# A gated mix of a spectral filter and a dense layer: first weights by halves, exchange writes on two queues, a new order, last stores moved

## The chip, the core and the metric

The kernel runs on one core of a Trainium2 chip. Five engines work side by side, each on its own list of instructions: TensorE (PE, matmuls; its weight loads are shown as PEld), VectorE (DVE), ScalarE (ACT), GpSimd (POOL) and SyncE (SP, which here only issues transfers and waits). Semaphores order them. The metric is the device time of one execution in microseconds (us). A profiled execution gives a trace; its span runs from the first to the last instruction.

## The reference

Inputs are bfloat16; S = 2048 rows, D = 512 columns, F = 1792 features. Two branches are mixed by a gate for each row:

```python
x = A_x
y = irfft2(rfft2(x) * (A_w_r + 1j * A_w_i))    # A: spectral filter
h = x @ B_w1 + B_b1
b = (h * tanh(softplus(h))) @ B_w2             # B: dense, Mish, dense
g = sigmoid((x * gate_w).sum(-1))
out = g * y + (1 - g) * b
```

Both branches read the same x.

## The kernel before

Everything is made as a list of tasks (`_Graph.add`), each with an engine, an assumed duration, what it reads and writes, and a priority. `schedule` (L203) simulates the engines with these durations and writes out one fixed order for each engine: among the tasks that could start within 0.03 us of the earliest, it takes the one of highest priority, with a small random term from `SEED`. Loads named in `LAND` (L334) are taken to land at the times in that table, others by size and a tail. `run_engine` (L918) then emits every engine's list in this order, with a semaphore wait ahead of a task for each thing that it needs. An engine never passes a waiting task.

The rows are 16 tiles of 128 (x's row 16p + t is partition p of tile t). The stages, with their lines:

- Loads (L487 to L523): x by tiles, w1 by feature tiles, constants, w2 and the filter W. SP and ACT issue the early ones in turn, POOL the bias, w2 and W, each queue in order.
- Warm-up matmuls on a zeroed buffer (L484), then transposes of x (L534) by way of PSUM, copied to xT by DVE (`evx`, L459).
- The dense branch. `mm1` (L855): 4 chunks of 4 row tiles, 14 feature tiles each, 4 matmuls of 128x512 for each feature tile; Mish on ACT (L862) empties the PSUM bank; `mm2` (L879): 14 matmuls for each row tile, done in two parts of 7. The banks that a chunk may use are in `DENSE` and `DENSE2`.
- The spectral branch. A1 (L572) and the combines into Abuf (L464) are a transform along d. `s1` (L603), four steps over 4 row tiles each, and its copies `e2` (L459 on DVE, L460 on ACT) into Ybuf are the first half of the one along rows. Exchange 1 writes Ybuf to a scratch in DRAM (`r1w`, 16 writes of 128 KB, L614) and reads it back with rows and partitions rearranged (`r1r`, 4 reads of 512 KB, L683), which waits for all writes. `s2` (L744), the filter's products on DVE (`wm`, L464) and sums on POOL (`wz`, L464), and `s2i` (L775) follow. Exchange 2 (L786, L791) and `s1i` and `a1i` (L804, L816) go back.
- A few filter columns have a chain of their own: `wcols` on POOL (L640), `rcw` on PE (L649), `weff` on DVE (L656), `wab1` and `wab2` on POOL (L662, L669); later `s2c` (L699), `crv`, `rcc` (L717).
- The gate (L621 on DVE, the power on POOL at L626) and the mix: `bev` (L837) scales mm2's result, `sum` adds; for the last two row tiles `fin` (L891) does both from PSUM. Stores go to SP's queue in pairs of tiles (L842), tile 14 alone, tile 15 in two halves of 256 columns (L894).

At the end SP waits for every load that it has not waited for yet (L943), then for the stores (L944).

Of the kernel before, what the change touches and what calls it, by code (L numbers as in the profile page):

```python
# [7 lines left out]
BF = mybir.dt.bfloat16  # L8
# [5 lines left out]
NT = 16  # L14
# [87 lines left out]


def _kind(name):
    return name.split("_")[0] if "_" in name else name.rstrip("0123456789")
# [47 lines left out]
class _Graph:  # L153
# [49 lines left out]
    def schedule(self):  # L203
# [13 lines left out]
        rng = np.random.RandomState(SEED)  # L217
        prio = {id(t): t.prio + OFFS.get(_kind(t.name), 0.0) + NOISE * rng.uniform(-1, 1) for t in tasks}
# [8 lines left out]
        while left:  # L227
# [92 lines left out]
NBF = 14  # L320
# [3 lines left out]
S1B = [(6, 7), (4, 5)]  # L324
A1B = (3, 4, 5, 6, 7)
SEED = 1294
NOISE = 0.02
OFFS = {}
SPEC = (3, 4, 5, 6, 7)
DENSE = {0: (0, 1, 2), 1: (0, 1, 2), 2: (0, 1, 7), 3: (0, 1)}  # L330
DENSE2 = {0: (0, 1), 1: (0, 1), 2: (0, 1, 2, 7), 3: (0, 1, 2, 7)}
NWARM = 16
COLD = 4.5
LAND = dict(ld_x0=2.8, ld_x1=3.0, ld_x2=3.5, ld_x3=3.7, ld_w1_0_0=5.6, ld_w1_0_1=5.2,  # L334
            ld_fd=5.8, ld_b1=4.7, ld_w1_2_0=7.6, ld_w1_2_1=7.2, ld_x4=9.1, ld_x6=8.4,
            ld_w1_4_0=10.6, ld_w1_4_1=9.9, ld_x8=11.9, ld_m10=13.2, ld_x12=14.5, ld_w1_8_0=15.2,
            ld_w1_8_1=15.9, ld_m11=17.3, ld_w1_12_0=17.7, ld_w1_12_1=18.1, ld_gw=18.4, ld_sm=20.1,
            ld_gd=20.3)
# [3 lines left out]
def _build(nc, A_x, A_w_r, A_w_i, B_x, B_w1, B_b1, B_w2, gate_w, out):  # L342
# [8 lines left out]
    with es:  # L351
# [76 lines left out]
        def dma(name, dst, src, reads=(), writes=(), nbytes=0, deps=(), is_out=False, prio=None, queue="sp", bw=380e3, tail=1.1, nd=128, issue=0.62):  # L428
            t = G.add(name, queue, 1.0 if queue == "pool" else issue, lambda e: e.dma_start(dst, src),  # L429
                      reads=reads, writes=writes, lat=tail, deps=deps, prio=prio)  # L430
            t.xfer = nbytes / bw
            t.isdma = True
            t.nd = nd
            if is_out:
                t.sem = out_sem
                n_out_dma[0] += 1
                t.semval = 16 * n_out_dma[0]
            else:
                t.sem = new_sem("d_" + name)
                t.semval = 16  # L440
            return t
# [28 lines left out]
        t_id = G.add("ident", "pool", 0.3, lambda e: e.affine_select(out=ident[:, :], in_=ident[:, :], pattern=[[1, 2], [2, 64]],  # L470
# [6 lines left out]
        G.add("wz", "dve", 0.3, lambda e: e.memset(act[:, 2, 0, :], 0.0), writes=["warm"])  # L477
        G.add("ebz", "pool", 0.2, lambda e: e.memset(b1f[:, 0:1], 0.0), writes=["b1z"])
        t_tab = G.add("table", "act", 1.3, lambda e: e.activation(b1f[:, 1:2], b1f[:, 0:1], AF.Mish), reads=["b1z"], writes=["b1t"], prio=0.0)

        pw = _Ps([6])
        tw = []
        for i in range(NWARM):
            tw.append(pe(f"warm{i}", mm(256), lambda e: e.matmul(ps[:, pw.bank, 0:256], act[:, 2, 0, 0:128], act[:, 2, 0, 0:256], start=True, stop=True),  # L484
                         reads=["warm"], alloc=pw if i == 0 else None, frees=[pw], prio=0.0, deps=tw[-1:]))
# [10 lines left out]


# [3 lines left out]
        ld_w1(0, 2, both)  # L501
        dma("ld_fd", FDs[:].rearrange("p r k -> p (r k)"), d_FD[:], writes=["FD"], nbytes=131072)
        dma("ld_b1", braw[:, :], B_b1.rearrange("(ft p) -> ft p", p=128), writes=["braw"], nbytes=3584, queue="pool", deps=[t_id])
        ld_w1(2, 4, both)
        ld_x(4, 6)
        ld_x(6, 8, "act")
        ld_w1(4, 8, both)
# [9 lines left out]
        for h in range(2):  # L517
            dma(f"ld_w2_{h}", w2_sb[:, 7 * h:7 * (h + 1), :], w2v[:, 7 * h:7 * (h + 1), :],
                writes=[("w2", h)], nbytes=128 * 7 * 1024, queue="pool", deps=[t_sm], bw=270e3)
        for i in range(2):  # L520
            for g in range(4):
                dma(f"ld_W{i}{g}", WT[32 * g:32 * g + 32, i, :, :].rearrange("p r k -> p (r k)"), Wv[i][g],
                    writes=[("W", i, g)], nbytes=32 * 8224, queue="pool", deps=[t_sm], bw=230e3)  # L523
# [3 lines left out]
        for t0, w in ((0, 1), (1, 1), (2, 2), (4, 2), (6, 2), (8, 2), (10, 2), (12, 2), (14, 2)):  # L527
            pt = _Ps(SPEC[::-1])
            def f_tr(e, t0=t0, w=w, pt=pt):
                ins = None  # L530
                for i in range(w):
                    for c in range(4):
                        o, d0 = (c * w + i) * 128, 256 * (c // 2) + c % 2
                        ins = e.transpose(psb[:, pt.bank, o:o + 128], xo[:, t0 + i, d0:d0 + 255:2], ident[:, :])  # L534
                return ins

            pe(f"tr{t0}", 4 * w * mm(128), f_tr, reads=[("x", t0 + i) for i in range(w)] + ["ident"], writes=[("ptr", t0)], alloc=pt)
            evict(f"evx{t0}", 512 * w, lambda t0=t0, w=w: xT[:, :, 128 * t0:128 * (t0 + w)],
                  lambda pt=pt, w=w: psb[:, pt.bank, 0:512 * w].rearrange("p (c j) -> p c j", c=4), rate=2.0,
                  reads=[("ptr", t0)], writes=[("xT", t0 + i) for i in range(w)], frees=[pt], engs=("dve",))  # L540
            if t0 == 2:
                pb = _Ps(SPEC[::-1])
                pe("tr_small", 0.1, lambda e, pb=pb: e.transpose(psb[:, pb.bank, 0:14].rearrange("p (a b) -> p a b", b=2), braw[0:14, :],
                                                                    ident[0:14, :].rearrange("p (b a) -> p a b", b=2)[:, 0:7, :]),
                   reads=["braw", "ident"], writes=["ptb"], alloc=pb)
                G.add("ev_small", "dve", 0.2, lambda e, pb=pb: e.tensor_copy(out=b1f[:, :], in_=psb[:, pb.bank, 0:14]),
                      reads=["ptb", "b1t"], writes=["b1f"], frees=[pb])
# [3 lines left out]
        for t in range(NT):  # L551
# [39 lines left out]
            if t % 4 == 3:  # L591
# [17 lines left out]
                for tp, p1 in zip((t - 3, t - 1), p1s):  # L609
                    evict(f"e2_{tp}", 1024, lambda tp=tp: Y1[:, 2 * tp:2 * tp + 4, :].rearrange("p (i b) k -> p i b k", b=2),  # L610
                          lambda p1=p1: ps[:, p1.sl, :].rearrange("p b (i k) -> p i b k", i=2),
                          reads=[("p1", tp)], writes=[("Y1", tp)], frees=[p1], prio=PR["sp"] + E2P, engs=("act",) if tp % 4 else ("dve",))
                    for rho in range(2):
                        dma(f"r1w{tp}{'ab'[rho]}", scr1_w[rho][:, 2 * tp:2 * tp + 4, :], Y1[rho::2, 2 * tp:2 * tp + 4, :], reads=[("Y1", tp)],  # L614
                            writes=[("scr1", tp, rho)], nbytes=64 * 4 * 512, prio=PR["sp"] + 1.0, tail=0.5, bw=300e3)
# [66 lines left out]
        for v in range(4):  # L682
            dma(f"r1r{v}", In2[:, 2 * v:2 * v + 2].rearrange("p u g k -> p (u g k)"),  # L683
                scr1_r[:, 2048 * v:2048 * v + 2048], reads=S1R, writes=[("In2", rho, 2 * v + i) for i in range(2) for rho in range(2)], deps=s1_tasks,
                nbytes=128 * 4096, prio=PR["sp"] + 1.0)
# [155 lines left out]
        def store(t):  # L841
            dma(f"out{t}", ov[:, t - 1:t + 1, :], xo[:, t - 1:t + 1, :], reads=[("o", t - 1), ("o", t)],  # L842
                nbytes=128 * 2048, is_out=True, prio=PR["fin"], tail=0.6)

        mm2s = {}
        for c in range(NCH):
            hb = c % 3
            G.cur_prio = PR["mm1"] - c
            for ft in range(NFT):
                pd = _Ps(DENSE[c])  # L850

                def f_mm1(e, c=c, ft=ft, pd=pd):
                    ins = None
                    for i in range(4):
                        ins = e.matmul(ps[:, pd.bank, :], w1_sb[:, i, 128 * ft:128 * (ft + 1)], xT[:, i, 512 * c:512 * c + 512],  # L855
                                       start=(i == 0), stop=(i == 3))
                    return ins

                pe(f"mm1_{c}_{ft}", 4 * mm(512), f_mm1, reads=[("xT", 4 * c + i) for i in range(4)] + [("w1", ft, 0), ("w1", ft, 1)],
                   writes=[("pm", c, ft)], alloc=pd, deps=mm2s.get(c - 3, ()), prio=PR["mm1"] - c - 0.06 * ft)  # L860
# [4 lines left out]
                      reads=[("pm", c, ft), "b1f"], writes=[("act", hb, ft)] + (["warm"] if hb == 2 and ft == 0 else []), frees=[pd], prio=PR["mish"])  # L865
            G.cur_prio = PR["mm2"] - c
            for tl in range(4):
                t = 4 * c + tl

                for part in range(2):  # L870
                    if part == 0 or t == NT - 1:
                        pd = _Ps(DENSE2[c])
                    cs_ = slice(256 * part, 256 * part + 256) if t == NT - 1 else slice(0, 512)
# [9 lines left out]
                    tk = pe(f"mm2_{t}_{part}", 7 * mm(512), f_mm2,  # L883
# [4 lines left out]
                    if t < NBF or (t < NT - 1 and part == 0):  # L888
                        continue
                    G.add(f"fin_{t}_{part}", "dve", dve_dur(256 if t == NT - 1 else 512, True),  # L890
# [4 lines left out]
                        nbytes=65536 * (1 if t == NT - 1 else 2), is_out=True, prio=PR["fin"], tail=0.6)  # L895
# [22 lines left out]
        def run_engine(ename, eobj):  # L918
            seen = {}
            for t in order[ename]:  # L920
                need = {}
# [18 lines left out]
            if ename == "sp":  # L940
                for t in G.tasks:
                    if t.isdma and t.sem is not out_sem and seen.get(t.sem.num, 0) < t.semval:
                        eobj.wait_ge(t.sem, t.semval)  # L943
# [67 lines left out]
```

## Time and profile before

| | us |
|---|---|
| three runs, median (lowest to highest) | 132.81 (132.79 to 133.22) |
| the profiled execution | 132.8 |
| its span | 131.1 |
| PE busy, share of the span | 124.9, 95% |
| first transposes on PE | 3.81 |
| first dense matmul (L855) | 7.29 |
| first step of s1 (L603) | 33.56 |
| first s2 (L744) | 54.45 |
| last s2i (L775) | 83.09 |
| first s1i (L804) | 93.59 |
| end of PE's last matmul | 128.15 |

The starts are those of the chain of work that ended last and of the timeline; all are us from the span's start. About 1.7 us of the execution lie outside the span. In the profile a line such as `7.29 1.89 PE L855 MATMUL ... x8 [0.79 <-DVE Tg L464]` gives the start, the time from the first start to the last end, the engine and line, the number of instructions, and in brackets the idle time before and what is thought to have ended it. A transfer's row gives the time from its issue to its landing.

### The profile page before, as it was taken

To read this page: it belongs to the slowest core of one execution; us is meant where nothing else is said; L and a number is where in the kernel's file an instruction comes from. 1 tells how busy PE (TensorE), PEld (TensorE's weight loads), DVE (VectorE), ACT (ScalarE), POOL (GpSimd) and SP (SyncE) were. 2 spreads that over 40 slices of the span, in tenths; PEclk is the share of its full clock that TensorE was granted. 3 is DMA by queue.
4 is the path that set the end of the run, shared out by engine and by line. 5 is a ranking of instruction groups with operands and counts; after the bars stand their busy time and mean duration, and the time that the engine had idled before them with its cause. 6 is when DMAs were issued, how large, how long until landed. Compare 5 with 4: busy or idle time off the path is not lost.

```text
span 131.1 us, 2497 instructions
## 1 busy us (share of the span) xinstructions
PE 124.9 (95%) x930; PEld 64.9 (50%) x947; DVE 89.3 (68%) x159; ACT 72.2 (55%) x119; POOL 58.3 (44%) x89
## 2 busy tenths in 40 slices
PE   6979999999999999999999999999999999999991
PEld 4646666544454444344343333344566555555580
DVE  0437989979797941296498994500267996899691
ACT  0437557898878787621236867922347741562420
POOL 6000009700020774059479979100019676879710
PEclk9999999999999999999999999999999999999999
DMA  3899964999956544956104050466910042022213
GB/s 106 258 293 420 386 209 81 368 287 228 223 138 199 171 123 109 336 235 250 75 26 134 3 160 5 143 177 171 404 70 0 0 156 84 5 80 83 80 46 116
DMA packets 16892, 21.09 MB, mean 161 GB/s; under 512 B 1200, under 2 KB 13360, under 8 KB 16496
## 3 DMA queue, kind: packets, MB, share of 16 engines
q1 hardware_dynamic: 14736, 15.95, 36.4%
q0 software_dynamic: 896, 3.94, 11.8%
q10 hardware_dynamic: 1248, 1.05, 2.6%
q8 instruction: 7, 0.11, 0.4%
q14 instruction: 5, 0.04, 0.1%
HBM read 14.64 MB, written 6.29 MB: 160 GB/s over the span
## 4 chain that ended last, share of the span: by engine, by line
PE 94%; issue 2%; DVE 1%; ACT 1%
PE ps L855 37%; PE ps L879 37%; PE ps L534 4%; PE ps L603 3%; PE ps L804 3%; PE ps L572 3%; PE ps L816 3%; PE ps L484 2%; PE ps L744 2%; PE ps L775 1%; ACT act L862 1%; DVE Tg L464 1%; DVE xo L891 0%; DVE act L477 0%; PE ps L699 0%
## 5 line engine op out<-in xcount | busy, mean ns | idle before, releaser
L855 PE MATMUL ps<-xT,w_sb 128*128 128x512 bf16 x214 | 51.0, 380 | 1.6 <-DVE Tg L464 0.8
L879 PE MATMUL ps<-w_sb,act 128*128 128x512 bf16 (+1 forms) x231 | 50.4, 366 | 0.4
L862 ACT ACTIVATE act<-ps,b1f 128x512 bf16<-128x512 f32 x56 | 38.5, 687 | 14.9 <-PE ps L855 14.1
L879 PEld LDWEIGHTS ps<-w_sb,act 128*128 128x128 bf16 x238 | 22.4, 98 | 22.1 <-issue 0.6
L855 PEld LDWEIGHTS ps<-xT,w_sb 128*128 128x128 bf16 x224 | 20.0, 98 | 25.5 <-ACT act L862 2.5
L464 POOL TENSOR_TENSOR Tg<-Qb 128x256 bf16<-128x256 f32 x29 | 21.6, 772 | 20.8 <-DVE Qb L827 20.8
L837 ACT ACTIVATE xo<-ps,omg 128x512 bf16<-128x512 f32 x14 | 9.6, 687 | 25.7 <-PE ps L879 22.9
L464 POOL TENSOR_TENSOR Zb<-Qb 128x510 bf16<-128x510 f32 x16 | 19.9, 1269 | 8.3 <-DVE Qb L464 8.3
L464 DVE TENSOR_TENSOR Qb<-ps,WT 128x1024 f32<-128x1024 f32 x16 | 18.8, 1218 | 6.3 <-PE ps L744 5.5
L827 DVE SCALAR_TENSOR_TENSOR Qb<-ps,gcol,Qb 128x256 f32<-128x256 f32 x32 | 13.6, 474 | 2.5 <-PE ps L816 2.5
L459 DVE CAST Ybuf<-ps 128x1024 bf16<-128x1024 f32 x8 | 9.8, 1220 | 4.6 <-PE ps L775 2.9
L464 DVE TENSOR_TENSOR Abuf<-ps,Tg 128x512 bf16<-128x512 f32 x16 | 10.3, 684 | 3.6 <-ACT Tg L579 3.6
L459 DVE CAST Zb<-ps 128x512 bf16<-128x512 f32 x7 | 4.7, 688 | 11.6 <-PE ps L804 11.2
L621 DVE SCALAR_TENSOR_TENSOR Tg<-xo,Tg 128x512 bf16<-128x512 bf16 x16 | 11.0, 686 | 0.3
L821 ACT ACTIVATE Qb<-ps,gcol 128x256 f32<-128x256 f32 x16 | 7.2, 470 | 7.0 <-PE ps L816 7.0
L429 POOL DMA_DIRECT2D w_sb<-in_B_w_dram x2 | 1.9, 974 | 16.9 <-DMA sm<-c_sm 16.9
L464 DVE TENSOR_TENSOR xo<-xo,Tg 128x512 bf16<-128x512 bf16 x14 | 9.3, 690 | 0.2 <-ACT xo L837 0.2
L460 ACT ACTIVATE Ybuf<-ps 128x1024 bf16<-128x1024 f32 x8 | 8.2, 1023 | 1.5 <-PE ps L603 1.2
L459 DVE COPY xT<-ps 128x1024 bf16<-128x1024 bf16 (+1 forms) x9 | 5.4, 627 | 4.6 <-PE ps L534 4.4
L640 POOL COPY wrv<-WT 128x2 bf16<-128x2 bf16 x2 | 0.4, 187 | 12.8 <-DMA WT<-in_A_w_i_dram 12.8
L804 PE MATMUL ps<-m1g,Abuf 128*128 128x128 bf16 x64 | 5.7, 219 | 0.0
L816 PE MATMUL ps<-GDs,Zb 128*128 128x128 bf16 x64 | 5.7, 219 | 0.0
(69 smaller groups left out, 88.4 us busy)
## 6 DMA issues: line engine op xcount, KB each, us to landing
Abuf<-scr SPq DMA_DIRECT2D x8, 512.0 KB, 5.4
scr<-Ybuf SPq DMA_DIRECT2D x16, 128.0 KB, 2.2
scr<-Ybuf SPq DMA_DIRECT2D x4, 512.0 KB, 3.2
w_sb<-in_B_w_dram POOLq DMA_DIRECT2D x2, 896.0 KB, 6.9
out_dram<-xo SPq DMA_DIRECT2D x7, 256.0 KB, 2.0
WT<-in_A_w_r_dram POOLq DMA_DIRECT2D x4, 257.0 KB, 9.1
WT<-in_A_w_i_dram POOLq DMA_DIRECT2D x4, 257.0 KB, 12.8
xo<-in_A_x_dram SPq DMA_DIRECT2D x2, 512.0 KB, 8.0
```

Source lines behind the costliest of these rows:

```text
L459: fs = {"dve": ("dve", dve_dur(n, rate=rate), lambda e: e.tensor_copy(out=dst(), in_=src())), "act": ("act", act_dur(n), lambda e: e.activ ...
L460: "act": ("act", act_dur(n), lambda e: e.activation(dst(), src(), AF.Copy))}
L464: f = lambda e: e.tensor_tensor(out=o(), in0=i0(), in1=i1(), op=op)
L621: lambda e, t=t: e.scalar_tensor_tensor(out=junk, in0=xo[:, t, :], scalar=1.0, in1=gwb, op0=ALU.mult, op1=ALU.mult, accum_out=gdot[:, t:t ...
L804: ins = e.matmul(ps[:, p4.bank, o:o + 128], T2r[:, 2 * t + bx, par::2], G1s[:, 16 * bx + t, :], start=True, stop=True)
L816: ins = e.matmul(ps[:, p5.bank, 128 * i:128 * i + 128], TT[:, sl, 2 * par + ri, :], GDs[:, i, :], start=True, stop=True)
L821: lambda e, t=t, sl=sl, p5=p5: e.activation(gC[:, sl, :].rearrange("p (i n) -> p i n", i=2), ps[:, p5.bank, :].rearrange("p (i n) -> p i n ...
L827: lambda e, t=t, sl=sl, p5=p5, o=o, op=op: e.scalar_tensor_tensor(out=st1[:, sl, o::2, :], in0=ps[:, p5.bank, :].rearrange("p (i n) -> p i ...
L837: G.add_multi(f"bev_{t}", [("act", act_dur(512, True), lambda e: e.activation(xo[:, t, :], ps[:, pd.bank, :], AF.Copy, scale=omg[:, t:t + ...
L855: ins = e.matmul(ps[:, pd.bank, :], w1_sb[:, i, 128 * ft:128 * (ft + 1)], xT[:, i, 512 * c:512 * c + 512], start=(i == 0), stop=(i == 3))
L862: lambda e, ft=ft, pd=pd, hb=hb: e.activation(act[:, hb, ft, :].rearrange("p (t a b) -> p t a b", t=4, b=2), ps[:, pd.bank, :].rearrange(" ...
L879: ins = e.matmul(ps[:, pd.bank, cs_], act[:, hb, ft, 128 * tl:128 * (tl + 1)], w2_sb[:, ft, cs_], start=(ft == 0), stop=(ft == NFT - 1))
```

## The change

- w1's first four feature tiles are loaded as four transfers of 128 KB with rows of 1 KB: the halves of d (a, b), each with one piece on SP and one on ACT. Before there were four of two feature tiles each, with rows of 512 bytes. The queues begin: SP x0, x2, a, FD, b, x4; ACT x1, x3, a, bias, b, x6. The bias load moves from POOL to ACT, and the second w1 piece of feature tiles 4 to 7 from ACT to SP.
- In chunk 0 the first four `mm1` tasks are split into a part of two matmuls on half a and one on half b; they may use banks 0 to 3.
- The transposes of tiles 2 and 3 get a task and a copy each. The warm-up has 17 matmuls on a constant tile, and no memset of its own.
- Of each pair of exchange 1's writes one goes to POOL's queue. `s1` may use banks 2 and 3 too; chunk 1 of the dense branch loses bank 2.
- The planner's assumptions change: LAND, longer tails, POOL issue times, the random term.
- Tile 15 ends with 384 and 128 columns; the store of its 384 and that of tiles 12 and 13 go to ACT's queue. SP's waits for old loads stand ahead of its first store.

In the order that this gives, PE runs 14 warm-ups, the transposes of tiles 0 to 3, 3 warm-ups, the a parts of two tiles, a b part (waiting for both b pieces), the bias transpose, another b part, and A1. The four steps of s1 have 8, 8 and 8 dense matmuls between them, rcw directly before the last, and 48 after it up to s2. On POOL four of exchange 1's writes stand ahead of wcols, two ahead of wab1, and two between wab2 and the gate's power.

```diff
-S1B = [(6, 7), (4, 5)]
+S1B = [(6, 7), (4, 5), (2, 3)]
-SEED = 1294
+SEED = 102926
-DENSE = {0: (0, 1, 2), 1: (0, 1, 2), 2: (0, 1, 7), 3: (0, 1)}
+DENSE = {0: (0, 1, 2), 1: (0, 1), 2: (0, 1, 7), 3: (0, 1)}
-NWARM = 16
-COLD = 4.5
-LAND = dict(ld_x0=2.8, ld_x1=3.0, ld_x2=3.5, ld_x3=3.7, ld_w1_0_0=5.6, ld_w1_0_1=5.2,
-            ld_fd=5.8, ld_b1=4.7, ld_w1_2_0=7.6, ld_w1_2_1=7.2, ld_x4=9.1, ld_x6=8.4,
+NWARM = 17
+COLD = 3.9
+LAND = dict(ld_x0=2.9, ld_x1=3.1, ld_x2=3.7, ld_x3=4.0, ld_w1_a0=4.9, ld_w1_a1=5.0,
+            ld_b1=6.6, ld_fd=5.6, ld_w1_b0=6.2, ld_w1_b1=6.2, ld_x4=9.0, ld_x6=9.0,
...
+        one_w, one_m = (nc.const_aps.tensor(1.0, (128, n), BF) for n in (128, 256))
...
+        def ld_w1c(h):
+            for e, q in enumerate(("sp", "act")):
+                dma(f"ld_w1_{'ab'[h]}{e}", w1_sb[:, 2 * h + e, 0:512], w1v[:, h, e, 0:512], writes=[("w1", f, h, e) for f in range(4)],
+                    nbytes=131072, queue=q, bw=330e3, tail=1.4)
...
-        ld_w1(0, 2, both)
+        ld_w1c(0)
+        dma("ld_b1", braw[:, :], B_b1.rearrange("(ft p) -> ft p", p=128), writes=["braw"], nbytes=3584, queue="act")
         dma("ld_fd", FDs[:].rearrange("p r k -> p (r k)"), d_FD[:], writes=["FD"], nbytes=131072)
-        dma("ld_b1", braw[:, :], B_b1.rearrange("(ft p) -> ft p", p=128), writes=["braw"], nbytes=3584, queue="pool", deps=[t_id])
-        ld_w1(2, 4, both)
+        ld_w1c(1)
         ld_x(4, 6)
         ld_x(6, 8, "act")
-        ld_w1(4, 8, both)
+        ld_w1(4, 8)
...
-        for t0, w in ((0, 1), (1, 1), (2, 2), (4, 2), (6, 2), (8, 2), (10, 2), (12, 2), (14, 2)):
+        for t0, w in ((0, 1), (1, 1), (2, 1), (3, 1), (4, 2), (6, 2), (8, 2), (10, 2), (12, 2), (14, 2)):
...
-                            writes=[("scr1", tp, rho)], nbytes=64 * 4 * 512, prio=PR["sp"] + 1.0, tail=0.5, bw=300e3)
+                            writes=[("scr1", tp, rho)], nbytes=64 * 4 * 512, prio=PR["sp"] + 1.0, tail=0.7, bw=290e3, queue=("sp", "pool")[rho], issue=0.64)
...
-                nbytes=128 * 2048, is_out=True, prio=PR["fin"], tail=0.6)
+                nbytes=128 * 2048, is_out=True, prio=PR["fin"], tail=0.6, queue="act" if t == NBF - 1 else "sp")
...
+                early = c == 0 and ft < 4
+                pd = _Ps((0, 1, 2, 3) if early else DENSE[c])
...
+                if early:
+                    t_a = pe(f"mm1_{c}_{ft}a", 2 * mm(512), lambda e, f=f_mm1: f(e, ds=(0, 1)), reads=xs + wr[0], alloc=pd, prio=PR["mm1"] - 0.06 * ft)
+                    pe(f"mm1_{c}_{ft}b", 2 * mm(512), lambda e, f=f_mm1: f(e, ds=(2, 3)), reads=xs + wr[1], writes=[("pm", c, ft)], deps=[t_a],
+                       prio=PR["mm1"] + 0.5 - 0.06 * ft)
...
-                    cs_ = slice(256 * part, 256 * part + 256) if t == NT - 1 else slice(0, 512)
+                    cs_ = slice(384 * part, 384 + 128 * part) if t == NT - 1 else slice(0, 512)
...
+                if ename == "sp" and t.isdma and t.sem is out_sem and not seen.get("loads"):
+                    seen["loads"] = 1
+                    for l in G.tasks:
+                        if l.isdma and l.sem is not out_sem and seen.get(l.sem.num, 0) < l.semval:
+                            seen[l.sem.num] = l.semval
+                            eobj.wait_ge(l.sem, l.semval)
...
-                for t in G.tasks:
-                    if t.isdma and t.sem is not out_sem and seen.get(t.sem.num, 0) < t.semval:
-                        eobj.wait_ge(t.sem, t.semval)
```

## The prediction

> **What bounds the kernel now.** I read the page's busy shares first, then the chain of waits in order of time, the timeline of the first 9 us, the table of stretches, the landing times of single transfers, and the last 3 us.
>
> ```profile
> PE 124.9 (95%) x930; PEld 64.9 (50%) x947; DVE 89.3 (68%) x159; ACT 72.2 (55%) x119; POOL 58.3 (44%) x89
> PE 94%; issue 2%; DVE 1%; ACT 1%
> ...
> 7.20:54.40 47.20, 46.74 (x346) 25.18 (x353) 34.16 (x72) 36.21 (x59) 12.89 (x24) 1.00 0.79 234
> 54.40:93.50 39.10, 38.52 (x296) 15.44 (x301) 23.84 (x22) 18.00 (x25) 21.74 (x25) 1.00 0.44 146
> 93.50:128.20 34.70, 34.37 (x265) 20.74 (x267) 28.26 (x59) 16.53 (x33) 21.59 (x29) 1.00 0.21 79
> ```
>
> The first number of a stretch is its length, the second PE's busy time. From 7.2 to 128.2 us PE is idle for 0.46 + 0.58 + 0.33 = 1.4 us in all, at the full granted clock. The change takes no matmul away, so another order can win at most that, and lose more. What is left is before 7.3 us and after 128.2 us.
>
> ```profile
> 3.81 1.92 PE L534 MATMUL ps<-ident,xo 128*128 128x128 bf16 x16
> 4.46 0.85 DVE L459 COPY xT<-ps 128x512 bf16<-128x512 bf16 x2 [3.27 <-PE ps L534]
> 5.77 0.69 DVE L459 COPY xT<-ps 128x1024 bf16<-128x1024 bf16 x1 [0.46 <-PE ps L534]
> 7.29 1.89 PE L855 MATMUL ps<-xT,w_sb 128*128 128x512 bf16 x8 [0.79 <-DVE Tg L464]
> ...
> 128.17 0.48 DVE L891 SCALAR_TENSOR_TENSOR xo<-ps,omg,Tg 128x256 bf16<-128x256 f32 x1 [0.60 <-PE ps L879]
> 128.68 0.33 SPq L429 DMA_DIRECT2D out_dram<-xo  x1
> ...
> L943 SPq EVENT_SEMAPHORE  x18: 27/28/28, 129.1 to 130.5; - x18
> ```
>
> At the start xT is complete at 5.77 + 0.69 = 6.46, yet the first dense matmul (L855) starts at 7.29. The engine named is DVE, but the wait is for w1: its piece on SP, issued at 1.71, took 5.5 us to land (7.2); ACT's, issued at 1.73, took 4.3 (6.1). At the end SP issues the last store at 128.68; it lands 1.5 us later, at 130.2. But SP passes 18 waits on old loads up to 130.5 and reaches the wait on the stores (L944) at 130.6: 0.4 us late.
>
> **The start.** One-tile copies take 0.85/2 = 0.425 us, so four from 4.46 on end at 6.16 and the first dense matmul can start at 6.3. It now needs only the first halves of w1, still third on their queues. Rows of 1 KB instead of 512 bytes halve the packets, and before the third pieces landed at 6.1 and 7.2. The kernel's own table of landings stands against the trace: x0 2.8 and 3.8, w1's first two 5.6 and 7.2, 5.2 and 6.1, the next two 7.6 and 8.8, 7.2 and 7.7, FD 5.8 and 7.9, x4 9.1 and 10.7, x6 8.4 and 8.5: the trace is 1.1 us later on average, between 0.1 and 2.1. The changed table's 4.9 and 5.0 for the first halves would then be 6.0 to 6.1, inside the copies' cover; without that cover every 0.1 us late costs 0.1.
>
> PE's order is: two tiles' first halves (4 matmuls), then one second half, which waits for both second pieces, the small bias transpose, another second half, the A1 matmuls. PE works in order, so a late second piece holds all of these, and ACT's first Mish and DVE's first combines behind them. A dense matmul costs 1.73/8 = 0.216 us (chain, the eight from 22.95). Four from 6.3 end at 7.16. The second pieces are fifth on SP and, after the tiny bias load, fifth on ACT. Earliest is where third pieces landed, 6.1; latest where the fifth on SP landed, 3.30 + 5.5 = 8.8. The table's 6.2 plus 1.1 is 7.3, near the middle, and I take it. The eight end at 7.3 + 4 x 0.216 + 0.11 (transpose, 5.78 to 5.89) = 8.3, against 7.29 + 1.73 = 9.0: **-0.7**. Ends: +0.75 (pieces at 8.8: 4 x 0.216 + 0.11 after it is 9.8), -0.9 (no wait). The one warm-up more, and an operand that needs no DVE memset, lie ahead of the x tiles, which land at 3.8 to 4.6 as before.
>
> **Two banks.** Chunk 1 of the dense layer loses bank 2, which exchange 1's stage now may use. The row for two banks is chunk 3 of before (banks 0, 1): 56 matmuls in 3.49 + 0.97 + 0.97 + 4.45 + 1.85 + 0.80 plus three gaps of 0.16 = 13.0 us, against 56 x 0.216 = 12.1. Restarts after short matmuls, which both orders have, are some six times 0.1; 0.3 is left. On three banks 44 took 9.6 against 9.5. So **+0.3**, between 0 and 0.9.
>
> **Exchange 1.** Its first stage (L603) has the same 92 dense matmuls ahead, then groups of 8, 8, 8 between its four steps (before 8, 12, 8 and 4). It began at 33.56; less 0.7, plus 0.2 of the bank cost, 33.1. Three steps of 0.99 and three groups of 1.83 put rcw (L649; before 42.90) at 41.5, the fourth step's end at 42.6, and s2 48 matmuls later: 9.6 (row for 44) + 0.86 = 10.5, so 53.1. At the same work before stood 54.45 - 0.86 = 53.6.
>
> Will the data be there? SP issued the 16 scratch writes serially, 0.62 us each; the last at 47.88 landed 2.2 later, the reads went at 50.39, the first landed 3.9 later (54.3). Now eight go to POOL. Four stand ahead of wcols: the last is ready at about 37.9 and issued by 39.2; W lands at 25.02 + 13.1 = 38.1; wcols' 0.7 us end at 39.9, before rcw at 41.5, so nothing waits. The last two stand behind wab1 and wab2, which ended 46.83 - 42.93 = 3.9 after rcw: 45.4. With 0.62 each (POOL's rows are 0.49 for 32 rows of W and 0.97 for w2) they are issued at 46.65. From issue's end to landing SP's took 2.2 - 0.62 = 1.6, POOL's bias load 3.6 - 0.78 = 2.8: 48.3 to 49.4. Plus 0.3 to the read's issue and 3.9: first read 52.5 to 53.7, PE there at 53.1. I take **+0.1**; ends 0 and 2.0 (issues of 0.97, and the pair before delaying wab1 by 0.7). Behind the last write POOL queues the gate's power, 2.94 us: over at 49.6, before 50.49.
>
> The Trainium skill weighs both sides of that in "DMA: Bandwidth & Descriptors". Section "Rules for kernel authors" says that spreading transfers over queues buys no bandwidth, only issue time; the trace agrees, with 0.62 us an issue against 2.2 to landing. Section "Anatomy of one DMA" fits POOL's path by 2.0 us plus bytes at 436 GB/s, 2.3 for these; counted from issue's end, as an estimate, the first read would land at 53.2.
>
> **After s2.** The order up to the second exchange is before's, with the chunk's last tile (0.86) moved behind the first s2: that much more room for the DVE and POOL chain, and s2c, which needs the last read (4.2 after the first: 58.5 against 54.3), comes 0.56 + 0.86 + 14 x 0.216 = 4.4 after s2's start. **0**, up to 0.3 either way from the new order of the last stage, by its 0.33 us of idle time.
>
> **The tail.** Waits on loads move ahead of the first store, where SP sat idle up to 14.2 us; without that cover they cost it some 2 us. -0.4. The last piece is 128 columns instead of 256: 512 columns take 0.69, 256 take 0.48, so 128 some 0.37: -0.1. A store of 256 KB landed in 2.0, 128 KB in 1.8, 64 KB in 1.5; 32 KB perhaps 1.45: -0.05. PE's 14 x 384 and 14 x 128 columns are before's 28 x 256, and the 384's finish (0.6) fits under the 14 short matmuls (14 x 0.056 = 0.78, from 16 transposes in 0.89). Two stores move to ACT, whose last work ended at 125.8. **-0.55**, between -0.3 and -0.65.
>
> One rule speaks against the last edit: the Trainium skill, same page, section "Specifications", says that below 512 bytes a transfer does a read-modify-write, and the last store now has 256-byte rows. No run here shows such a store; the page gives no price.
>
> **Sum**, against the profiled execution's 132.8 (span 131.1; the shown median is 132.81): -0.7 + 0.3 + 0.1 - 0.55 = -0.85, so **131.95 us**.
>
> **Rivals.** *Exchange 1 on POOL becomes the bound.* For: two queue steps of POOL behind wab2, and PE has nothing but s2 there. Against: three us are gained ahead of it (last step ends 42.6, before 44.84). It decides once the first read lands after 54.05, 0.95 past PE; at 54.6 PE waits 1.5, and 132.8 - 0.7 + 0.3 + 1.5 - 0.55 = 133.35: slower. *The second pieces come late* (8.2): the start is lost, 4 x 0.216 + 0.11 after 8.2 is 9.2, +0.15; exchange 1 then waits for nothing, and only the tail is left: 132.8 + 0.15 + 0.3 - 0.55 = 132.7. For it speaks that SP's pieces landed 1.1 us after ACT's; against it the halved packets. *It all works*: no wait for the second pieces (-0.9), no bank cost, none at s2, tail -0.65: 131.25. For it: ACT's Mish (0.69) is shorter than a tile's 0.86, so two banks can do.
>
> **Chances.** Forecast 0.5, all works 0.2, late pieces 0.2, POOL the bound 0.1. A measurement of this kernel tells some 0.3% (0.4 us) from no change. Below 132.4: the forecast's 0.48, all of 0.2 and 0.02 of the late pieces; above 133.2: 0.02 of these and 0.07 of POOL's; the rest is the same: 0.70, 0.21, 0.09. The range 131.2 to 133.0 leaves out part of POOL's case and the far end of "all works".
>
> **What would show it.** First dense matmul near 6.3; a gap before the fifth no longer than 0.2; s2 near 53.1 with DMA as its releaser by at most 0.2; POOL's last two writes issued by 46.7; SP at the stores' wait before they land; end of PE to end of span 2.4 instead of 2.9. I am wrong if s2 starts after 54, or the eighth dense matmul ends after 9.

## The result and the profile after

The changed kernel took 132.11 us (median; 131.22 to 132.97), the kernel before, beside it, 132.89 (132.44 to 134.28): a ratio of 0.9926, 95% interval 0.9905 to 0.9947. In three further comparisons the medians were 132.03, 131.72 and 131.82, with ratios of 0.9923 to 0.9928. Over all 42 runs the changed kernel's median is 131.91, and its runs scatter by 1.75 us. The profiled execution, 131.42 us with a span of 129.7, is one of its faster ones.

The page of the changed kernel, busy shares and the chain's shares by engine:

```profile
PE 126.3 (97%) x948; PEld 64.3 (50%) x948; DVE 87.8 (68%) x157; ACT 73.1 (56%) x120; POOL 63.8 (49%) x97
...
PE 86%; DMA 5%; POOL 4%; DVE 1%; ACT 1%; issue 1%; SPq 0%
```

Its stretches, cut as before (length, PE's busy time, then the other engines, granted clock, DMA share, GB/s):

```profile
7.20:54.40 47.20, 47.14 (x360) 24.91 (x359) 35.28 (x74) 36.34 (x59) 18.41 (x32) 1.00 0.82 245
54.40:93.50 39.10, 39.10 (x293) 15.77 (x292) 22.64 (x23) 18.44 (x26) 21.76 (x25) 1.00 0.42 136
93.50:128.20 34.70, 33.90 (x260) 19.66 (x258) 27.11 (x57) 16.80 (x34) 22.43 (x30) 1.00 0.20 74
```

PE's idle time in the first two stretches reads 0.06 us and none now, for 0.46 and 0.58 before, but that is no gain. The page of before has 930 matmuls for 947 weight loads, so 17 matmul records are missing; this page has 948 for 948. Where one is missing the rows show a hole of 0.05 or 0.16 us, and before's trace has exactly 17 of these between its first and its last dense matmul and no other. The repeats of the changed kernel below come with and without such holes, and their stretches are equally long. The 0.80 of the third stretch is the time behind PE's last matmul, which ends at 127.41. The start, in the timeline of PE:

```profile
6.07 1.47 PE L861 MATMUL ps<-xT,w_sb 128*128 128x512 bf16 x6 [0.22 <-DVE xT L459]
7.47 0.18 PE L548 MATMUL ps<-ident,braw 14*128 14x14 bf16 x1
7.59 0.61 PE L861 MATMUL ps<-xT,w_sb 128*128 128x512 bf16 x2
8.03 1.06 PE L577 MATMUL ps<-FDs,Tg 128*128 128x128 bf16 x16
```

The first dense matmul starts 1.2 us earlier (6.07 for 7.29), released by the copy and no longer by w1. The second pieces landed at 6.45 and 6.77, before the fifth matmul needed them at 6.95: the row of six takes 1.47, much as in a run further down in which all pieces were there before the first (1.45). So PE did not wait for the second pieces here. A1 follows at 8.03, before at 9.01. Exchange 1 lies on the chain of waits now, read in order of time:

```profile
40.77 1.24 POOL scr L429 x2
...
42.02 0.33 POOL ch L667
...
42.66 3.06 POOL wab L674 x7
45.72 0.65 POOL scr L429
46.37 2.21 DMA scr<-Ybuf
...
48.66 4.08 DMA Abuf<-scr
...
52.78 0.63 PE ps L749 x16
```

This is the queue that the prediction described: the last two writes stand behind the wab operations, the last is issued at 46.37 and lands 2.21 later, the read lands at 52.74, and s2 (L749) starts at 52.78. That 9% of the span lies on the chain does not mean that it costs anything: PE's last dense matmul ahead of s2 ended when the read landed. What it costs shows in the next table.

The tail: DVE's last piece and the last store in the timeline, then the rows of SP's waits on old loads in the changed kernel.

```profile
127.44 0.35 DVE L904 SCALAR_TENSOR_TENSOR xo<-ps,omg,Tg 128x128 bf16<-128x128 f32 x1 [0.16 <-PE ps L892]
127.82 0.33 SPq L429 DMA_DIRECT2D out_dram<-xo  x1
```
```profile
L939 SPq EVENT_SEMAPHORE  x18: 27/28/28, 89.4 to 95.6; - x18
```

The waits are over at 95.6, so none of them stands between the landing at 129.27 and the end at 129.68, 0.41 later (before: 130.22 and 131.06, 0.84 later).

Every trace can be cut at the same five points, each the start of a first (or last) record on PE: A1's first matmul (L577 after, L572 before), s1's first, s2's first, the last matmul of all, and the end of the span. All times are us; the records' starts lie up to 0.2 ahead of the chain's.

| trace | A1 starts | A1 to s1 | s1 to s2 | s2 to last matmul | last matmul to end | end |
|---|---|---|---|---|---|---|
| before | 9.01 | 24.48 | 20.89 | 73.48 | 3.20 | 131.06 |
| after | 8.03 | 24.67 | 20.08 | 74.40 | 2.50 | 129.68 |
| after_again | 8.30 | 24.48 | 20.02 | 74.40 | 2.49 | 129.69 |
| after_third | 8.56 | 24.48 | 19.97 | 74.40 | 2.49 | 129.90 |
| after_fourth | 8.49 | 24.48 | 20.29 | 74.40 | 2.49 | 130.15 |
| e_sp_only | 8.07 | 24.60 | 20.87 | 74.40 | 2.50 | 130.44 |
| e_waits_last | 8.42 | 24.48 | 19.97 | 74.40 | 3.07 | 130.34 |
| e_early_w | 8.60 | 24.48 | 19.97 | 74.40 | 2.49 | 129.94 |
| e_s2_later | 8.51 | 24.48 | 20.83 | 74.01 | 2.49 | 130.32 |
| before_waits_first | 8.54 | 24.60 | 20.89 | 73.49 | 2.77 | 130.29 |
| e_third_a | 9.68 | 24.05 | 20.07 | 74.40 | 2.50 | 130.70 |
| e_both | 8.77 | 24.05 | 19.97 | 74.40 | 2.49 | 129.68 |
| e_whole | 11.49 | 24.48 | 20.19 | 74.40 | 2.51 | 133.07 |
| e_whole_warm | 9.73 | 24.48 | 20.03 | 74.40 | 2.50 | 131.14 |

In the two traces of the old order 0.86 us of matmuls stand ahead of s2 that the new order runs behind it, so 20.89 compares with 20.03 + 0.86, and 73.48 with 74.34. With that, the 1.38 us between the two profiled spans are: A1 0.98 earlier, A1 to s1 0.19 longer, s1 to s2 0.05 longer, s2 to the last matmul 0.06 longer, the tail 0.70 shorter. Where PE never waits, the middle is the same to 0.01 us from one execution to another; three places move: the start, the wait at s2 (what a trace of the new order has above 19.97), and the tail. In three traces A1 to s1 is also 0.12 to 0.19 longer, since transposes wait there for a late load of x; in e_third_a and e_both it is 0.43 shorter, since two dense matmuls have moved ahead of A1.

### The profile page after: what moved, and what is told of

Its sections match the earlier page's. It is cut to its first block, busy times and chain, and to the rows that moved or that the text cites. A ratio compares the mean times of both kernels' runs of the same rounds, so it can differ in the third digit from the quotient of the medians.

```text
span 129.7 us, 2516 instructions
## 1 busy us (share of the span) xinstructions
PE 126.3 (97%) x948; PEld 64.3 (50%) x948; DVE 87.8 (68%) x157; ACT 73.1 (56%) x120; POOL 63.8 (49%) x97
## 4 chain that ended last, share of the span: by engine, by line
PE 86%; DMA 5%; POOL 4%; DVE 1%; ACT 1%; issue 1%; SPq 0%
PE ps L892 37%; PE ps L861 29%; DMA Abuf<-scr 3%; PE ps L809 3%; PE ps L577 3%; PE ps L821 3%; PE ps L539 3%; PE ps L484 2%; POOL wab L674 2%; PE ps L608 2%; PE ps L749 2%; PE ps L780 2%; DMA scr<-Ybuf 2%; POOL scr L429 1%; DVE xT L459 1%; ACT Ybuf L460 1%
## 5 line engine op out<-in xcount | busy, mean ns | idle before, releaser
L861 PE MATMUL ps<-xT,w_sb 128*128 128x512 bf16 x224 | 52.8, 380 | 0.2 <-DVE xT L459 0.2
L892 PE MATMUL ps<-w_sb,act 128*128 128x512 bf16 (+2 forms) x238 | 51.6, 367 | 0.0
L892 PEld LDWEIGHTS ps<-w_sb,act 128*128 128x128 bf16 x238 | 21.9, 98 | 22.3 <-issue 0.6
L464 POOL TENSOR_TENSOR Tg<-Qb 128x256 bf16<-128x256 f32 x30 | 22.4, 773 | 19.9 <-DVE Qb L832 19.6
L459 DVE CAST Zb<-ps 128x512 bf16<-128x512 f32 x6 | 4.1, 688 | 11.5 <-PE ps L809 11.2
L429 POOL DMA_DIRECT2D scr<-Ybuf x8 | 5.1, 645 | 12.0 <-ACT Ybuf L460 12.0
L464 DVE TENSOR_TENSOR xo<-xo,Tg 128x512 bf16<-128x512 bf16 x14 | 8.6, 644 | 0.6 <-POOL Tg L464 0.6
L821 PEld LDWEIGHTS ps<-GDs,Zb 128*128 128x128 bf16 x64 | 4.6, 98 | 2.6 <-DVE Qb L832 0.3
```

Source lines behind the costliest of these rows:

```text
L429: t = G.add(name, queue, issue, lambda e: e.dma_start(dst, src), reads=reads, writes=writes, lat=tail, deps=deps, prio=prio)
L459: fs = {"dve": ("dve", dve_dur(n, rate=rate), lambda e: e.tensor_copy(out=dst(), in_=src())), "act": ("act", act_dur(n), lambda e: e.activ ...
L464: f = lambda e: e.tensor_tensor(out=o(), in0=i0(), in1=i1(), op=op)
L821: ins = e.matmul(ps[:, p5.bank, 128 * i:128 * i + 128], TT[:, sl, 2 * par + ri, :], GDs[:, i, :], start=True, stop=True)
L892: ins = e.matmul(ps[:, pd.bank, cs_], act[:, hb, ft, 128 * tl:128 * (tl + 1)], w2_sb[:, ft, cs_], start=(ft == 0), stop=(ft == NFT - 1))
```

## The experiments

Two theories stood against each other. S: how late A1 starts travels one to one to the end. E: exchange 1's reads set the pace, and what the start wins is lost at s2. Edits are to the changed kernel unless said otherwise; the lines stand right behind `order = G.schedule()`, so that all else keeps its place.

**The changed kernel again** (after_again, after_third and after_fourth, each beside the experiments of its group).

> The changed kernel once more, as the partner of the three beside it. Median near 132.1, with single executions between 131.2 and 133.0 (22 runs so far), where the kernel before lay between 132.4 and 133.4 but for one. Theory E (exchange 1 sets the pace): PE reaches s2 just as the first read lands (52.74 in the profile of after), so an execution of 132 or more shows s2 later than 52.8 with DMA as its releaser and the same first dense matmul near 6.1. Rival S (the start): such an execution shows the first dense matmuls or a transpose held by a load, and s2 later by the same amount without a wait of its own.

> The changed kernel as the partner of the three beside it: median near 132.05, executions from 131.3 to 132.7. If its trace is of a slow execution, theory E wants the first read's landing at the place of the loss, rival S a load of the start.

> The changed kernel again, beside the three that follow, on one chip. Earlier medians 131.72 to 132.11. Both theories, S (how late PE's first A1 matmul starts travels one to one to the end) and E (exchange 1's reads set the pace): 131.9, within 0.4. By S the time from A1's first matmul to the first step of s1 is again 24.5 us, and the span ends 96.9 after that step.

Measured: 132.03, 131.72 and 131.82 us; ratios 0.9928 [0.9904, 0.9952], 0.9923 [0.9903, 0.9943], 0.9925 [0.99, 0.9951]. The table shows A1 between 8.30 and 8.56 and a wait at s2 of 0.05, 0 and 0.32. The second pieces of w1 landed between 6.59 and 7.34.

**All of exchange 1's writes on SP** (e_sp_only).

```diff
+        mv = [t for t in order["pool"] if t.name.startswith("r1w")]
+        order["pool"] = [t for t in order["pool"] if not t.name.startswith("r1w")]
+        for t in mv:
+            t.eng = "sp"
+            k = [u.name for u in order["sp"]].index(t.name[:-1] + "a")
+            order["sp"].insert(k + 1, t)
```

> Exchange 1's writes all on SP's queue again, each right behind its partner; every other engine's order as in after. SP then issues four writes of 0.66 from 43.4, the last at 45.4, landed at 47.6, where POOL's last landed at 48.57. The first read would land at 51.8, 0.9 before PE reaches s2. Theory E: the late executions go, the median falls by 0.3 to 0.7 towards 131.5 and the spread shrinks. Rival S: median and spread stay as after's (132.1). If POOL's queue is what the gain rests on, it is slower by up to 0.5.

Measured: 132.30 us, ratio 0.995 [0.993, 0.9969], 0.27 slower than the changed kernel beside it, whose interval it overlaps. In its timeline, SP's issues and then PE's row at s2:

```profile
34.82 12.43 SPq L429 DMA_DIRECT2D scr<-Ybuf  x16
```
```profile
53.54 0.62 PE L749 MATMUL ps<-Abuf,sm 64*32 64x512 bf16 x16 [0.83 <-DMA Abuf<-scr]
```

Sixteen issues of 0.62 would take 9.9 us; three took 1.55, 0.97 and 1.24, and the last went out at 46.63, no earlier than POOL's 46.37. The read then took 4.46 to land and PE waited 0.83. So SP alone brought no gain, where E expected one. The two queues were worth some 0.8 us between these traces, although POOL's half stands behind wab, and 0.27 between the medians, which the intervals do not separate.

**The waits for old loads back at the end** (e_waits_last), and, from the other side, **the kernel before with these waits ahead of its first store and nothing else** (before_waits_first). The lines are those of the second; the first takes them back in the changed kernel.

```diff
             for t in order[ename]:
+                if ename == "sp" and t.isdma and t.sem is out_sem and not seen.get("loads"):
+                    seen["loads"] = 1
+                    for l in G.tasks:
+                        if l.isdma and l.sem is not out_sem and seen.get(l.sem.num, 0) < l.semval:
+                            seen[l.sem.num] = l.semval
+                            eobj.wait_ge(l.sem, l.semval)
...
             if ename == "sp":
-                for t in G.tasks:
-                    if t.isdma and t.sem is not out_sem and seen.get(t.sem.num, 0) < t.semval:
-                        eobj.wait_ge(t.sem, t.semval)
                 eobj.wait_ge(out_sem, 16 * n_out_dma[0])
```

> SP's waits on old loads behind its last store again, all else as after. From the rows of before (18 waits from 129.06 to 130.60, 1.55 us) SP would reach the stores' wait 1.55 after its last issue ends at 128.15, so at 129.7, where the last store lands at 129.27: slower than after by 0.4, whichever of E and S holds. If the waits cost nothing it equals after.

> The kernel before with nothing but SP's waits on old loads moved ahead of its first store. The trace of before has SP at the stores' wait 0.4 after the last landing (130.6 against 130.2): 0.4 faster than before by the prediction's tail term. The run with the waits last in after came out equal to after, though its trace too shows SP 0.5 late; if that holds here, no gain at all.

Measured: e_waits_last 132.05 us (131.81 to 132.28), the changed kernel beside it 132.03; before_waits_first 132.34, ratio 0.9961 [0.9944, 0.9979], 0.54 under the kernel before. The row of the waits in e_waits_last:

```profile
L956 SPq EVENT_SEMAPHORE  x18: 27/28/28, 128.3 to 129.8; - x18
```

The last store had landed at 129.35, and SP was still passing waits until 129.88: 0.53 us late, and the tail in the table is 0.57 longer. The fastest of its six runs is 0.38 above the fastest of the six beside it, but the medians don't show it; the start scatters by half a microsecond, and six runs are too few against that. From the other side the same edit showed in the median.

**Two of POOL's writes ahead of wab2** (e_early_w) and **s2 one dense tile later** (e_s2_later): more room for the read, by an earlier read or a later PE.

```diff
+        names = [t.name for t in order["pool"]]
+        mv = [t for t in order["pool"] if t.name in ("r1w12b", "r1w14b")]
+        rest = [t for t in order["pool"] if t not in mv]
+        k = [t.name for t in rest].index("wab2")
+        order["pool"] = rest[:k] + mv + rest[k:]
```
```diff
+        names = [t.name for t in order["pe"]]
+        k = min(names.index("s2_00"), names.index("s2_01"))
+        nxt = order["pe"].pop(k + 2)
+        assert nxt.name.startswith("mm1_2")
+        order["pe"].insert(k, nxt)
```

> POOL's order only: exchange 1's last two writes go out ahead of wab2's seven small operations instead of behind them. In after's trace they were ready at 43.4 and issued at 45.66 and 46.37; now POOL issues them from about 43.4, beside SP's last two, all land by 46.7, and the first read lands near 50.8, two us before PE comes to s2 at 52.75. wab2 and the gate's power end some 2 us later (49 and 51), both before they are needed (the power at 57). Theory E: median near 131.5, executions within 0.4 of it. Rival S: as after_third, 132.05 with the same spread. If a later wab2 or power holds something, slower than after_third.

> PE's order only: the last dense tile of chunk 2 (4 matmuls, 0.86) stands ahead of the first two s2 tasks again, as in the kernel before. PE comes to s2 at 53.6, 0.85 after the first read's landing in after's profile. Theory E: lateness up to 0.85 no longer costs PE anything at that place: 131.5 to 131.7 and a smaller spread; but the DVE and POOL chain to the last s2i has 0.86 less room, and if that binds it comes out at 132.0 or above. Rival S: 132.05, spread unchanged.

Measured: 131.70 us (131.27 to 131.97) and 132.06, the changed kernel beside them 131.72. With early writes the read landed at 52.09, and s2 started at 53.05 when PE came: 0.96 us of room, and nothing won, since in the trace beside it PE had not waited either. With s2 later, 0.86 of matmuls went ahead of it, and only 0.39 came back by the last matmul. In that trace the chain of waits runs over DVE's products and POOL's sums from 54.31 to 64.46, and PE's s2 matmuls at 57.85 and 64.50 start when these release them: this chain had less than 0.86 of room.

**The first dense matmul waits for all four pieces** (e_whole), and **the same with twelve more warm-up matmuls ahead of it** (e_whole_warm, whose lines stand behind those of e_whole).

```diff
+        first = {t.name: t for t in G.tasks}
+        first["mm1_0_0a"].deps += [first["ld_w1_b0"], first["ld_w1_b1"]]
```
```diff
+        k = order["pe"].index(first["mm1_0_0a"])
+        for _ in range(12):
+            t = _Task("more", "pe", 0.1, first["warm0"].fn)
+            order["pe"].insert(k, t)
```

> The first dense matmul waits for all four pieces of w1's first tiles instead of the two first ones; loads, queues and orders as after. In after's profile the last of the four landed at 6.77 and the first dense matmul began at 6.07: PE would start 0.7 later. Theory E: little of it is seen, since PE would wait for s2's data anyway unless the first stage of exchange 1 is later by as much too (it is, by 0.7, as it stands behind PE): slower by about 0.7 under both; 0 would say that the halves do nothing for the end.

> The first dense matmul waits for all four pieces, as in the run at 134.0, and twelve more warm-up matmuls of 256 columns stand ahead of it (12 x 0.108 = 1.3 us of the gap of 2.3 us in which PE was idle there). If the clock that fell in the gap made the loss there, the dense matmuls behind it take 0.216 each and the median is 132.4 to 132.9, 0.4 to 1.0 above the changed kernel (the wait itself). If the late pieces alone made it, 133.7 or more again.

Measured: e_whole fell into two groups, 131.84 and 132.25 at a mean granted clock of 1.0, and 133.90 to 134.84 (four runs) at 0.987; the changed kernel beside it lay between 131.43 and 132.64. In its profiled execution, of the second group, PE's timeline, and then the stretches (length, PE busy, granted clock, DMA):

```profile
5.49 0.49 PE L484 MATMUL ps<-const-bfloat16-1.0 128*128 128x256 bf16 x3
8.19 2.72 PE L861 MATMUL ps<-xT,w_sb 128*128 128x512 bf16 x6 [2.21 <-DMA w_sb<-in_B_w_dram]
```
```profile
6.00:8.10 2.10, 0.00 (x0) 0.92 0.94 295
8.10:9.00 0.90, 0.81 (x3) 0.50 1.01 328
9.00:12.00 3.00, 3.00 (x18) 0.64 1.06 424
```

The granted clock fell to half in the gap of 2.21 us, and the six matmuls behind it took 2.72 instead of 1.47. With the gap filled, e_whole_warm's 12 runs lay between 132.18 and 133.24 (median 132.78), all at a clock of 1.0. PE's timeline in its profiled execution:

```profile
7.79 1.45 PE L861 MATMUL ps<-xT,w_sb 128*128 128x512 bf16 x6 [0.86 <-DMA w_sb<-in_B_w_dram]
```

So the clock made the 134. What the wait itself costs is less certain. e_whole_warm is 0.96 slower than the changed kernel beside it, about the 0.86 of the four matmuls that no longer run ahead of the second pieces, and beside the old kernel no clear gain is left (ratio 0.9982 [0.9962, 1.0001]). But the profiled executions of both runs had late second pieces (the last at 8.05 and 7.65, against 6.77 to 7.34 in the changed kernel), and e_whole's two runs at the full clock lie among the changed kernel's own. So starting on half the weights is worth between nothing that can be measured and 0.96 while the clock holds, and some 2 us where it falls; what the rows of 1 KB and the one-tile copies add was not tried alone.

**The third a part ahead of the first b part** (e_third_a), and **that with the early writes** (e_both).

```diff
+        pn = {t.name: t for t in order["pe"]}
+        order["pe"].remove(pn["mm1_0_2a"])
+        order["pe"].insert(order["pe"].index(pn["mm1_0_0b"]), pn["mm1_0_2a"])
```

> The a part of the third feature tile stands ahead of the first b part on PE: the b pieces are needed two matmuls, 0.43 us, later. S: executions in which the b pieces land late get up to 0.4 shorter, those in which they land in time stay, so the median falls by 0.1 to 0.3 against the changed kernel beside it and the range narrows at its upper end. E: whatever the start wins is lost at s2, whose wait grows by as much; median the same within 0.1.

> The third a part ahead, and exchange 1's last two writes on POOL ahead of wab2. S: as with the a part alone, median 0.1 to 0.3 below the changed kernel. E: the room won at the exchange (the read landed 1.0 us ahead of PE in the run with early writes) lets the earlier start through, so only this one of the two gains, by 0.3 or more; best of all, 131.5 or less.

Measured: 131.76 us (131.44 to 132.44) and 131.59 (131.41 to 131.81), the changed kernel beside them 131.82; ratios to the kernel before 0.992 [0.989, 0.995] and 0.9905 [0.9882, 0.9928]. The a part alone missed what S expected: its median fell by 0.06, and its range, 1.00 us, is hardly narrower than the 1.20 beside it. Its profiled execution, one of the two slowest of seven, shows why in PE's timeline:

```profile
6.03 1.47 PE L861 MATMUL ps<-xT,w_sb 128*128 128x512 bf16 x6 [0.23 <-DVE xT L459]
8.60 0.59 PE L861 MATMUL ps<-xT,w_sb 128*128 128x512 bf16 x2 [1.10 <-DMA w_sb<-in_B_w_dram]
```

Here ACT's b piece, issued at 2.91 like the others, landed at 8.46, 2 us behind SP's, and 0.43 of cover is little against that. The span of 130.70 follows from that start: the rest of its row is that of the other traces. e_both has the lowest median and the narrowest range of all; the intervals still overlap, so that it beats the changed kernel is likely, not shown.

What the theories made of it: the columns of the table add up to the end by themselves; what speaks for S is that the stretches behind A1 hardly change, 24.48 and 74.40 in most rows of the new order, so that a late A1 is made up for nowhere. E is right for a part: the wait at s2 was 0.11, 0.05, 0 and 0.32 in the four traces of the changed kernel, and gone in both with early writes. In all four the first read landed between 0.07 us before and 0.27 after PE's coming (s1's start plus 19.97): there is no room to spare. All 12 runs of these two lie at or below 131.97, of the changed kernel's 42 only 23. Whether the upper half comes from late reads or from late pieces of w1 is open: of such runs no trace of the changed kernel was taken.

The traces show a third source of late starts that neither theory names. In three of the twelve traces of the new order (after_again, after_fourth and e_both) PE runs the last transposes and the three warm-ups behind them at half pace, 0.213 us a warm-up; in the other nine these take 0.11. The row of the three warm-ups and that of the first dense matmuls, in after, after_again and after_fourth:

```profile
5.36 0.50 PE L484 MATMUL ps<-const-bfloat16-1.0 128*128 128x256 bf16 x3
6.07 1.47 PE L861 MATMUL ps<-xT,w_sb 128*128 128x512 bf16 x6 [0.22 <-DVE xT L459]
```
```profile
5.62 0.80 PE L484 MATMUL ps<-const-bfloat16-1.0 128*128 128x256 bf16 x3
6.34 1.47 PE L861 MATMUL ps<-xT,w_sb 128*128 128x512 bf16 x6
```
```profile
5.54 0.85 PE L484 MATMUL ps<-const-bfloat16-1.0 128*128 128x256 bf16 x3
6.27 1.74 PE L861 MATMUL ps<-xT,w_sb 128*128 128x512 bf16 x6
```

In after_again the transposes end later, and with them the copies; the first dense matmul and A1 come 0.27 later. In after_fourth the first dense matmul comes 0.20 later and the first two still run at about half pace, 0.40 and 0.31 us apart instead of 0.22: A1 is 0.46 later. The pieces of w1 were there in time in both. Only in after_third, where A1 is 0.53 later, was it w1: the first pieces held the first dense matmul (landed 6.28, PE at 6.41), the second pieces the fifth. The profile's granted clock reads 1.00 in these stretches all the same, so the pace is read from the matmuls' own times. No run was made to steer when the full pace comes, so its cause stays open.

## Why the prediction was right

The forecast was 131.95; the first median was 132.11, the median of all its runs 131.91. By its steps:

- *What bounds the kernel.* The 1.4 us that PE was said to idle between 7.2 and 128.2, the most that another order could win, were a misreading: 1.2 of them are the holes of the 17 missing records, the rest lies ahead of the first dense matmul and behind the last. By the starts of its matmuls PE waited some 0.3 us there (0.24 for banks, below, and 0.06 at s2). That most of what is left lies before 7.3 and after 128.2 was right.
- *The start, -0.7.* The first dense matmul came when it was said to (6.07 to 6.41, for 6.3), and the eight were done at 8.19 by the chain in the profile, for 8.3. But the forecast lets the second pieces end the stage, at 7.3. They landed at 6.8 to 7.3, and PE waited for them in one trace of the four, after_third, by 0.2; in the others the first dense matmul's start and PE's pace set the end. A1 came 0.98 earlier than in the profile of before, in the repeats 0.45 to 0.71. The size depends on which execution of before it is set against, which the prediction did not weigh: with an unchanged start, before_waits_first began A1 at 8.54.
- *Two banks for chunk 1, +0.3.* This is the step that failed: the term measured 0. A1 to s1, which holds the first half of that chunk, takes 24.48 in the old order and in the new; the groups of eight between s1's steps, which hold nearly all the rest, take 1.83, as the group of eight before did. The price in chunk 3 is real: there four and five dense tiles follow each other on two banks, and in before's trace a third (or fifth) tile starts 0.08 late three times, 0.24 in all, each time just behind ACT's Mish that empties its bank. The first of the three, in the row of its weight load:

```profile
71.06 0.55 PEld L855 LDWEIGHTS ps<-xT,w_sb 128*128 128x128 bf16 x4 [0.41 <-ACT act L862]
```

What failed is carrying it over. In the order that the planner writes for the new kernel, A1's groups, s1's steps and two tiles of chunk 2 on bank 7 stand between chunk 1's tiles. No more than two of them follow each other, and none waits. The 0.19 in one trace has another cause: x's tiles 6 and 7 landed late, at 9.92, and held the transposes until 9.97.
- *Exchange 1, +0.1.* Right: 0.05 in the profiles' comparison, 0 to 0.32 of wait. The last two writes were issued by 47.0 (forecast 46.65), s2 came at 52.78 (53.1). These two POOL writes took 0.63 to 0.71 to issue and 2.2 from issue to landing, as before's last ones on SP: near the lower end that the prediction gave for the landing (48.57, for 48.3 to 49.4). The estimate that it made from the Trainium skill's "DMA: Bandwidth & Descriptors", section "Anatomy of one DMA", 2.3 counted from issue's end, was too long for these two; counted from the issue's start it agrees. (The "three us" given against POOL as the bound are 44.84 - 42.6 = 2.2 by its own rows.)
- *After s2, 0.* Measured +0.06, in every trace the same.
- *The tail, -0.55.* Measured -0.64 from PE's end to the span's end (2.91 to 2.27). The waits alone were given -0.4: the trace of before_waits_first shows -0.43 and its median -0.54. The last store, 32 KB with rows of 256 bytes, landed in 1.45 us as forecast, before's 64 KB with rows of 512 in 1.54: of the read-modify-write that the same page, section "Specifications", tells of below 512 bytes nothing shows here.

So it was in part luck that the medians met the number: two terms were off and cancelled, as the banks cost nothing and the start won less in the repeats (0.45 to 0.71) than in the profile. Term by term the profiled execution is nearer to the rival "it all works" (no wait for the second pieces, no bank cost, almost none at s2, a tail of -0.65; 131.25 forecast, 131.42 measured). The medians lie 0.5 to 0.9 above the rival's number. In the traces of the repeats A1 is later by PE's late pace or late pieces of w1, and one waits 0.32 at s2; the forecast has one execution in mind and no scatter of these. POOL as the bound did not come. Second pieces as late as the rival's 8.2 came once in twelve traces, in e_third_a (8.46).

## What to carry to other kernels

Cut every trace at a few fixed points on the bounding engine before explaining a difference: stretches that agree to 0.01 us leave only the places that move, and a share of the chain of waits is no price. Compare the counts of matmuls and weight loads before reading holes as idle time. A wait read from one stage is a price in another only where the same tasks follow each other. Split an early load so that the first matmuls need half of it, and keep PE occupied until they start: beside the wait, a gap can cost the clock. A wait that needs nothing late belongs ahead of the last store's, where its engine is idle.

## What the hardware showed that was not expected

- Behind 5 us of warm-ups and transposes with small holes, a gap of 2.2 us on PE came with half the granted clock: in e_whole's trace it fell at 7.76, 1.8 us after PE had stopped, and was back at 1.00 at 11.18. It was traced once; four of the six runs have the mean clock of that trace, 0.987, and none of the twelve with the gap filled. The Trainium skill, "TensorE: Matmul & The Clock Gate", section "Why this matters for your kernels", warns of gaps above some 3 us; here a shorter one was enough.
- Loads issued at the same time land differently from one execution to the next: ACT's second piece of w1, always issued at 2.91 and of 128 KB, landed between 6.54 and 8.46 in these traces. Where PE waited 1.10 for it, in e_third_a, nothing behind A1 made that up.
- PE reached its full pace at very different times: in e_whole_warm the transposes took 56 ns each from 3.75 us on, in after_fourth 107 ns until 5.5 and dense matmuls were slow until 6.9, behind the same fourteen warm-ups.
- SP's issues of the scratch writes, 0.62 us as a rule, take 1.0 to 1.6 now and then; POOL's eight took 0.62 to 0.71.
